# First pair's q on ScalarE's queue and in a bank of its own, raw weights behind the first finished x, last tile's transposes in a row

## Chip, core and metric

The kernel runs on one core of a Trainium2 chip. The metric is the device time of one execution in microseconds, as the median of several runs.

## What is computed

Attention with a soft cap on the scores, for 4 batches of 12 heads with 448 tokens of 64 features, and behind it two two-layer MLPs over the 1792 tokens (768 to 2048 to 768 features), all in fp32:

```python
scores = cap * tanh(q @ k.T / sqrt(64) / cap)
attn   = exp(scores - max) / (sum(exp(scores - max)) + 1e-9)
x = attn @ v                                  # 4 x 12 x 448 x 64, then as 1792 x 768
h = maximum(x @ w1, 0);  x = (h * h) @ w2
h = x @ w3;              out = (h * sigmoid(1.702 * h)) @ w4
```

## The kernel before

`bounded_cap` serves caps up to 40, which the inputs have; `any_cap` is a second version behind a branch on the flag `over`, which isn't taken here. All engines run in the order in which the code is written (`in_order`), so the order of the source is the order of the queues.

**Attention** goes over 24 pairs of heads. Time is cut in steps T, eight to a pair: `PLAN` says at which step, counted from the pair's own first, each piece of it is emitted. `load_pair` (step -17) fetches k and q of a pair on SP's queue, `load_v` (-9) v. `prep_k` and `prep_q` transpose them on TensorE against `ident` into the PSUM pool `ps_x`, which has a single bank, and split them in a high and a low part: k by ScalarE (copy) and VectorE (subtract) to `kk`, q by two VectorE passes to `qq`. `scores`, `tanhs`, `exps` and `pv` follow for four chunks of keys; the last chunk (`TAIL`) holds the 64 left over keys of both heads. `take_x` and `divide` make x, which POOL's queue writes to `xs`. k is kept in two buffers `kz`, whose unused rows `emit_const` clears.

**Weights.** The MLP's weights come as raw 8-byte words. For each of 11 chunks within attention, two loads (`wraw`, POOL's queue) are each followed by a join (ScalarE into `sx`, then VectorE's shift to `wy`), and then by sums (four VectorE operations) and writes to `wsa` or `wsb` (POOL's queue). `weight_group` puts these into a list, three loads ahead; `weight_slot`, called at the steps of `ATT_WORK`, takes one join or one sum from it, with the loads that follow. The group is opened at step 2:

```python
if T == 2:
    weight_group(ATT_CHUNKS)
if T in ATT_WORK:
    weight_slot()
...
ATT_WORK = tuple(10 + 11 * n // 2 for n in range(33))
```

The list is taken up at the first slot, step 10, where the three loads at its head are emitted ahead of the first join. On POOL nothing but its constants is queued ahead of them, so they leave as soon as these are set.

**MLPs.** From there TensorE works through products (`product`, L1094) of weights `wh`, `wl` with `form`. The last result tile of the second MLP is transposed back in `result` with four TensorE transposes into one bank, each followed by a copy and an output DMA, on VectorE and SP's queue or on ScalarE and its queue in turn.

Of the kernel before, what the change touches and what calls it, by code (L numbers as in the profile page):

```python
# [8 lines left out]
F32 = mybir.dt.float32  # L9
# [667 lines left out]
@with_exitstack  # L677
def bounded_cap(ctx, tc, q, k, v, cap, w1, w2, w3, w4, out):

# [59 lines left out]
    sx = const.tile([P, KD, P], I32, name="sx")  # L739
    kz = [kz_p.tile([P, KW], F32, name=f"kz{i}") for i in range(2)]  # L740
    v1 = [kz_p.tile([P, 2 * TAIL + 1, 2, D], F32, name=f"v1{i}") for i in range(VB)]
# [7 lines left out]
    def emit_const():  # L749
        nc.vector.memset(kz[0][:32], 0.0)  # L750
        nc.gpsimd.memset(kz[1][:32], 0.0)
        nc.sync.dma_start(out=capt, in_=cap.rearrange("(o n) -> o n", o=1).to_broadcast([P, 1]))
# [6 lines left out]
        nc.vector.reciprocal(qs, acap)  # L759
        nc.vector.tensor_scalar(ecap, acap, CAP_MAX, None, ALU.min)  # L760
        nc.vector.tensor_scalar(qs, qs, float(D) ** -0.5, None, ALU.mult)


    pairs = [(b, p) for b in range(B) for p in range(NP)]
    raw, vst, prep, pps, sc, et, pvp, x32 = ({} for _ in range(8))

    def halves():
        for j in range(2):
            yield j, slice(64 * j, 64 * j + 64), slice(64 * (1 - j), 64 * (1 - j) + 64)

    def load_pair(b, p):
        kt = kz[p % 2].rearrange("p (c h d) -> p c h d", h=2, d=D)
        qt = ld.tile([CP, NCH, 2, D], F32, tag="q", name="qt")
        ka, kb, qa, qb = (
            src[b, 2 * p + j].rearrange("(p c) d -> p c d", c=NCH) for src in (k, q) for j in range(2)
        )
# [7 lines left out]
    def transposed(t, name):  # L784
        n = KW if name == "kps" else S
        ps = ps_x.tile([P, 512], F32, tag="x", name=name)
        for c in range(NCH):
            nc.tensor.transpose(
                ps[:, c:n:NCH], t[:, c].rearrange("p h d -> p (h d)"), ident[: n // NCH, : n // NCH]
            )  # L790
        return ps[:, :n]

    def load_v(b, p):
        va, vb = v[b, 2 * p], v[b, 2 * p + 1]
        vt = vst[b, p] = v1[(b * NP + p) % VB]
        tt = vt[:, 2 * TAIL]
        Q_LOAD.dma_start(out=vt[:, 0 : 2 * TAIL : 2, 0], in_=va[64:].rearrange("(c p) d -> p c d", p=P))
        Q_LOAD.dma_start(out=vt[:, 1 : 2 * TAIL : 2, 1], in_=vb[: TAIL * P].rearrange("(c p) d -> p c d", p=P))
        Q_LOAD.dma_start(out=tt[64:, 0], in_=va[:64])
        Q_LOAD.dma_start(out=tt[:64, 1], in_=vb[TAIL * P :])  # L800

    def prep_k(b, p, step):
        if step == 0:
            pps[b, p] = transposed(raw[b, p][1], "kps")
            return
        ps = pps[b, p]
        if step == 1:
            kk = qk_p.tile([P, 2, KW], F32R, tag="kk", name="kk")
            prep[b, p] = [None, kk]
            a_.activation(kk[:, 0, :], ps, AF.Copy)  # L810
        else:
            kk = prep[b, p][1]
            v_.tensor_tensor(kk[:, 1, :], ps, f32(kk[:, 0, :]), ALU.subtract)

    def prep_q(b, p, step):
        if step == 0:
            pps[b, p] = transposed(raw.pop((b, p))[0], "qps")
            return
        ps = pps[b, p]
        if step == 1:  # L820
            qq = prep[b, p][0] = qk_p.tile([P, 2, S], F32R, tag="qq", name="qq")
            v_.tensor_scalar(qq[:, 0, :], ps, qs, None, ALU.mult)  # L822
        else:
            qq = prep[b, p][0]
            v_.scalar_tensor_tensor(qq[:, 1, :], ps, qs, f32(qq[:, 0, :]), ALU.mult, ALU.subtract)

    def scores(b, p, c):
        qq, kk = prep[b, p]
        ps = sc[b, p, c] = ps_s.tile([P, 2, 512], F32, tag="s", name="sps")
        tail = c == TAIL  # L830
        cols = slice(0, P) if tail else slice((c + 1) * P, (c + 2) * P)
        if tail:
# [24 lines left out]
    def pv(b, p, c):  # L857
# [22 lines left out]
    def divide(b, p):  # L880
# [375 lines left out]
    def result(l, c, row, col, d, y):  # L1256
# [183 lines left out]
def softcap_attention_mlp_mlp(ctx, tc, q, k, v, cap, w1, w2, w3, w4, out):  # L1440

    nc = tc.nc
    pool = ctx.enter_context(tc.tile_pool(name="flag", bufs=1))
    c = pool.tile([1, 2], F32, name="capsize")
    over = pool.tile([1, 1], I32, name="over")
    nc.sync.dma_start(out=c[:, 0:1], in_=cap.rearrange("(o n) -> o n", o=1))
    nc.vector.tensor_scalar(c[:, 1:2], c[:, 0:1], -1.0, None, ALU.mult)
    nc.vector.tensor_tensor(c[:, 0:1], c[:, 0:1], c[:, 1:2], ALU.max)
    nc.vector.tensor_scalar(over, c[:, 0:1], CAP_MAX, None, ALU.is_gt)
    bounded_cap(tc, q, k, v, cap, w1, w2, w3, w4, out)  # L1450
    flag = nc.values_load(over, min_val=0, max_val=1)
# [32 lines left out]
```

## Time and profile before

| | us |
|---|---|
| median of three runs | 1115.71 |
| the three runs | 1114.51, 1115.71, 1116.39 |
| the profiled execution | 1114.16 |
| its span | 1112.4 |
| TensorE busy | 1069.3 (96%) |
| VectorE busy | 863.2 (78%) |
| ScalarE busy | 722.6 (65%) |

The profile is of one execution. A timeline row gives the start and the duration of one instruction (or of several merged ones, "x4"), its engine (PE is TensorE, PEld its weight loads, DVE VectorE, ACT ScalarE, POOL GpSimd, SPq and ACTq the DMA issues of SP and ScalarE), its line in the kernel, the tile it writes and the tiles it reads. What stands in brackets is how long the engine was idle before it, and what ended that. Matmul ends are modelled, so a busy TensorE isn't one at its peak.

### The profile page before, as it was taken

To read this page: it belongs to the slowest core of one execution; us is meant where nothing else is said; L and a number is where in the kernel's file an instruction comes from. 1 tells how busy PE (TensorE), PEld (TensorE's weight loads), DVE (VectorE), ACT (ScalarE), POOL (GpSimd) and SP (SyncE) were. 2 spreads that over 40 slices of the span, in tenths; PEclk is the share of its full clock that TensorE was granted. 3 is DMA by queue.
4 is the path that set the end of the run, shared out by engine and by line. 5 is a ranking of instruction groups with operands and counts; after the bars stand their busy time and mean duration, and the time that the engine had idled before them with its cause. 6 is when DMAs were issued, how large, how long until landed. Compare 5 with 4: busy or idle time off the path is not lost.

```text
span 1112.4 us, 15612 instructions
## 1 busy us (share of the span) xinstructions
PE 1069.3 (96%) x5119; PEld 887.4 (80%) x5119; DVE 863.2 (78%) x1173; ACT 722.6 (65%) x1131; POOL 276.6 (25%) x414
## 2 busy tenths in 40 slices
PE   4999999999999999999999999999999999999997
PEld 2555554556999999989998998999799879998996
DVE  2788889999667987876699769778894875569854
ACT  3999998997667656466685655667555455565541
POOL 2222233322342013122210322443022410001033
PEclk9999999999999999999999999999999999999999
DMA  6798999856878467688964876898343543333442
GB/s 168 199 242 225 247 272 249 217 179 218 264 272 279 135 227 259 208 264 286 309 220 156 270 270 197 281 319 287 119 152 106 195 140 114 101 113 117 136 127 65
DMA packets 158860, 228.23 MB, mean 205 GB/s; under 512 B 80898, under 2 KB 111746, under 8 KB 158770
## 3 DMA queue, kind: packets, MB, share of 16 engines
q0 software_dynamic: 33696, 122.28, 33.7%
q1 hardware_dynamic: 124818, 104.75, 32.4%
q8 instruction: 42, 0.69, 0.3%
q14 instruction: 48, 0.39, 0.1%
q10 hardware_dynamic: 256, 0.11, 0.0%
HBM read 166.53 MB, written 60.56 MB: 204 GB/s over the span
## 4 chain that ended last, share of the span: by engine, by line
PE 59%; DVE 14%; issue 8%; DMA 5%; ACT 4%; POOL 1%; DVEq 0%; ACTq 0%; POOLq 0%
PE pb L1094 28%; PE pa L1094 27%; DVE form L1103 3%; DMA wf<-wsa 3%; DVE wl L1071 3%; PE vps L867 2%; PE sps L841 1%; DMA out_dram<-o 1%; DVE ct L882 1%; ACT sx L942 1%; DVE g L1215 1%; DVE g L1296 1%; DVE qu L1296 1%; ACT e L851 1%; ACT e L855 1%
## 5 line engine op out<-in xcount | busy, mean ns | idle before, releaser
L1094 PE MATMUL pa<-form,wh 128*128 128x448 f32 x1536 | 439.7, 367 | 7.1 <-DVE form L1103 5.8
L1094 PE MATMUL pb<-form,wh 128*128 128x448 f32 x1152 | 329.4, 367 | 2.0 <-DVE form L1103 1.1
L1094 PEld LDWEIGHTS pa<-form,wh 128*128 128x128 f32 x1536 | 288.9, 188 | 34.3 <-DVE form L1103 7.4
L1094 PE MATMUL pa<-form,wl 128*128 128x448 f32 x768 | 282.4, 368 | 5.4 <-DVE wl L1071 5.3
L1070 ACT ACTIVATE wh<-wf 128x384 fp32r<-128x384 f32 (+1 forms) x392 | 211.3, 560 | 66.2 <-DMA wf<-wsa 27.1
L1071 DVE TENSOR_TENSOR wl<-wf,wh 128x384 fp32r<-128x384 f32 (+1 forms) x392 | 225.4, 607 | 27.7 <-ACT wh L1070 22.8
L1094 PEld LDWEIGHTS pb<-form,wh 128*128 128x128 f32 x1152 | 216.5, 188 | 22.3 <-DVE form L1103 1.8
L1094 PE MATMUL pb<-form,wl 128*128 128x448 f32 x576 | 210.8, 366 | 0.0
L1094 PEld LDWEIGHTS pa<-form,wl 128*128 128x128 f32 x768 | 144.5, 188 | 20.2 <-DVE wl L1071 8.3
L867 PE MATMUL vps<-e,v 128*128 128x448 f32 (+1 forms) x384 | 148.1, 552 | 2.3 <-DVE x L878 2.2
L1276 POOL DMA_DIRECT2D out_dram<-o x92 | 57.9, 636 | 253.9 <-DVE o L1274 250.6
L1094 PEld LDWEIGHTS pb<-form,wl 128*128 128x128 f32 x576 | 108.3, 188 | 9.1
L1103 DVE TENSOR_TENSOR form<-g,form 128x1344 fp32r<-128x1344 f32 (+1 forms) x72 | 100.7, 1399 | 8.5 <-ACT form L1102 7.8
L841 PE MATMUL sps<-qq,kk 64*128 64x448 f32 (+1 forms) x504 | 92.6, 419 | 0.9 <-DVE qq L822 0.9
L867 PEld LDWEIGHTS vps<-e,v 128*128 128x128 f32 (+1 forms) x384 | 59.6, 189 | 42.4 <-issue 26.0
L855 ACT ACTIVATE e<-e,ecap 128x896 f32<-128x896 f32 x96 | 91.0, 948 | 1.9
L1293 ACT ACTIVATE qu<-pb 128x448 f32<-128x448 f32 x88 | 47.5, 540 | 68.7 <-PE pb L1094 65.1
L946 DVE SCALAR_TENSOR_TENSOR wy<-wraw,sx 128x768 int32<-128x768 int32 (+1 forms) x68 | 61.7, 908 | 37.3 <-ACT sx L942 37.3
L851 ACT ACTIVATE e<-sps 128x896 f32<-128x896 f32 x96 | 78.0, 813 | 19.2 <-PE sps L841 18.6
L841 PEld LDWEIGHTS sps<-qq,kk 64*128 64x128 f32 (+1 forms) x504 | 50.0, 190 | 46.6 <-ACT kk L810 13.0
L1102 ACT ACTIVATE form<-g 128x1344 fp32r<-128x1344 f32 (+1 forms) x72 | 85.8, 1192 | 2.0 <-DVE g L1254 1.9
L882 DVE RECIPROCAL ct<-ct 128x448 f32<-128x448 f32 x24 | 70.7, 2945 | 0.0
(91 smaller groups left out, 1001.1 us busy)
## 6 DMA issues: line engine op xcount, KB each, us to landing
wf<-wsa SPq DMA_DIRECT2D x224, 192.0 KB, 3.9
wf<-wsb SPq DMA_DIRECT2D x168, 256.0 KB, 3.2
wraw<-in_moe_w_in_dram POOLq DMA_DIRECT2D x32, 766.5 KB, 7.2
wraw<-in_moe_w_out_dram POOLq DMA_DIRECT2D x48, 383.2 KB, 6.0
wsa<-wy POOLq DMA_DIRECT2D x32, 384.0 KB, 4.3
wsb<-wy POOLq DMA_DIRECT2D x24, 384.0 KB, 4.4
wsa<-ws POOLq DMA_DIRECT2D x16, 384.0 KB, 3.4
wraw<-in_moe_w_out_dram POOLq DMA_DIRECT2D x24, 255.5 KB, 5.1
```

The lines of the kernel that those rows point to most:

```text
L841: nc.tensor.matmul(ps[:, u, :S], x, y, start=all(t[0] != u for t in todo[:n]), stop=all(t[0] != u for t in todo[n + 1 :]),)
L851: a_.activation(e, chunk(c, sc.pop((b, p, c)))[:, :, :S], AF.Tanh)
L855: a_.activation(e, e, AF.Exp, scale=ecap)
L867: nc.tensor.matmul(pvp[b, p][j][:, :S], x.rearrange("p a d -> p (a d)"), t, start=c == 0, stop=c == TAIL,)
L882: v_.reciprocal(ct, ct)
L946: v_.scalar_tensor_tensor(y[:, : 2 * n].bitcast(I32), words(I32)[:, :, :, 0], 13, sx[:, : 2 * n], ALU.logical_shift_right, ALU.bitwise_or,)
L1070: a_.activation(x, src, AF.Copy)
L1071: later.append(lambda: v_.tensor_tensor(y, src, f32(x), ALU.subtract))
L1094: nc.tensor.matmul(ps[:, :S], a[:, kk % 4, :], r, start=(s in (1, 5) and kk == 0 and n == 0), stop=(kk == ks - 1 and n == 2), skip_group_c ...
L1102: a_.activation(f[:, 0, :n, :], src, AF.Copy)
L1103: later.append(lambda: v_.tensor_tensor(f[:, 1, :n, :], src, f32(f[:, 0, :n, :]), ALU.subtract))
L1276: nc.gpsimd.dma_start(out=out[b * S : (b + 1) * S, m * P + 32 * j : m * P + 32 * j + 32].rearrange("(c p) d -> p c d", p=32), in_=o[32 * j ...
```

## The change

- `load_pair` of the first pair issues q on ScalarE's queue; k and v are fetched in other pieces (k's and v's first 384 tokens as 128 x 3, the last 64 by themselves), and step -17 becomes -18. The cap is loaded once, on ScalarE's queue, and `over` is computed from `acap`.
- The first pair's preparation is written out in `attn_start`: q's transposes go first, into a bank of `ps_m`, then k's into `ps_x`. T starts at -10 instead of -17.
- The weight group opens at step 15 with its first three loads (`weight_loads`), behind the first `divide` at step 14, and `ATT_WORK` is 26 + 5n instead of 10 + 5.5n.
- The last tile's four transposes stand one behind the other; then VectorE and ScalarE copy two columns of blocks each and issue one DMA each.

```diff
 def load_pair(b, p):
+    kt = kz[p % 2]
     qt = ld.tile([CP, NCH, 2, D], F32, tag="q", name="qt")
-    Q_LOAD.dma_start(out=kt[16:, :, 0, :], in_=ka)
-    Q_LOAD.dma_start(out=kt[32:, :, 1, :], in_=kb[:96])
-    Q_LOAD.dma_start(out=kt[:16, :, 1, :], in_=kb[96:])
-    Q_LOAD.dma_start(out=qt[:, :, 0, :], in_=qa)
-    Q_LOAD.dma_start(out=qt[:, :, 1, :], in_=qb)
+    queue = nc.scalar if (b, p) == pairs[0] else Q_LOAD
+    for j in range(2):
+        Q_LOAD.dma_start(out=kt[:, :TAIL, j], in_=k[b, 2 * p + j, :MAIN].rearrange("(p c) d -> p c d", c=TAIL))
+    for j, r, o in halves():
+        Q_LOAD.dma_start(out=kt[r, TAIL, j], in_=k[b, 2 * p + j, MAIN:])
+    for j in range(2):
+        queue.dma_start(out=qt[:, :, j], in_=q[b, 2 * p + j].rearrange("(p c) d -> p c d", c=NCH))
...
 def prep_q(b, p, step):
     if step == 0:
-        pps[b, p] = transposed(raw.pop((b, p))[0], "qps")
+        bank = ps_m if (b, p) == pairs[0] else None
+        qps[b, p] = transposed(raw[b, p][0], "qps", bank)
         return
...
+    def attn_start():
+        for f, step in ((prep_q, 0), (prep_k, 0), (prep_q, 1), (prep_k, 1), (prep_q, 2), (prep_k, 2)):
+            f(*pairs[0], step)
...
+    def weight_loads():
+        while work and work[0][0].__name__.startswith("load"):
+            f, *a = work.pop(0)
+            f(*a)
...
         for j in range(NCH):
-            at = slice(P * j, P * j + P)
-            nc.tensor.transpose(ps[:CP, at], y[:, CP * j : CP * j + CP], ident)
-            (v_.tensor_copy, a_.copy)[j % 2](o[:CP, at], ps[:CP, at])
-            (nc.sync, nc.scalar)[j % 2].dma_start(
-                out=out[b * S + CP * j : b * S + CP * j + CP, m * P : m * P + P], in_=o[:CP, at]
+            nc.tensor.transpose(ps[:CP, P * j : P * j + P], y[:, CP * j : CP * j + CP], ident)
+        for j, copy, queue in ((0, v_.tensor_copy, nc.sync), (2, a_.copy, nc.scalar)):
+            at = slice(P * j, P * j + 2 * P)
+            copy(o[:CP, at], ps[:CP, at])
+            queue.dma_start(
...
-    T = -17
+    T = -10
+    nc.scalar.dma_start(out=capt, in_=cap.rearrange("(o n) -> o n", o=1).to_broadcast([P, 1]))
+    load_pair(*pairs[0])
     emit_const()
...
-        if T == 2:
+        if T == 15:
             weight_group(ATT_CHUNKS)
+            weight_loads()
...
-ATT_WORK = tuple(10 + 11 * n // 2 for n in range(33))
+ATT_WORK = tuple(26 + 5 * n for n in range(33))
```

How the instructions stand then, at three places. On TensorE at the start of the program (kps and qps are the transposes of k and q, sps the scores), before:

```order
L788 MATMUL kps<-ident,kz_117 128x128 x4
L788 MATMUL qps<-ident,qt 128x112 x4
L841 MATMUL sps<-qq,kk 128x448 x6
L788 MATMUL kps<-ident,kz_118 128x128 x4
L841 MATMUL sps<-qq,kk 128x448 x6
L788 MATMUL qps<-ident,qt 128x112 x4
```

and now:

```order
L789 MATMUL qps<-ident,qt 128x112 x4
L789 MATMUL kps<-ident,kz_112 128x128 x4
L840 MATMUL sps<-qq,kk 128x448 x6
L789 MATMUL kps<-ident,kz_113 128x128 x4
L840 MATMUL sps<-qq,kk 128x448 x6
L789 MATMUL qps<-ident,qt 128x112 x4
```

q's transposes of the first pair have moved ahead of k's; the second pair's stand where they stood. On POOL, behind its constants (wraw are raw weights, wsa and xs the DRAM tiles of the weights and of x), before:

```order
L756 MEMSET sx 128x768
L930 DMA wraw<-in_moe_w_in_dram 128x6x1022 x3
L961 DMA wsa_124<-wy 128x2x384
L930 DMA wraw<-in_moe_w_in_dram 128x6x1022
L884 DMA xs<-x_303 128x448
L930 DMA wraw<-in_moe_w_in_dram 128x6x1022
```

and now:

```order
L753 MEMSET sx 128x768
L883 DMA xs<-x_291 128x448
L938 DMA wraw<-in_moe_w_in_dram 128x6x1022 x3
L883 DMA xs<-x_380 128x448
L969 DMA wsa_119<-wy 128x2x384
L938 DMA wraw<-in_moe_w_in_dram 128x6x1022
```

The first x is now written ahead of the first raw loads, and the second ahead of the first joined weights. On SP at the start (qt, kz and v are the tiles of q, k and v), before:

```order
L1446 DMA capsize<-in_cap_dram 1x1
L752 DMA capt<-in_cap_dram 128x1
L777 DMA kz_117<-in_k_dram 112x4x64
L778 DMA kz_117<-in_k_dram 96x4x64
L779 DMA kz_117<-in_k_dram 16x4x64
L780 DMA qt<-in_q_dram 112x4x64
L781 DMA qt<-in_q_dram 112x4x64
L1451 TENSOR_LOAD over
L1451 ISA x2
L797 DMA v_119<-in_v_dram 128x3x64
```

and now:

```order
L778 DMA kz_112<-in_k_dram 128x3x64 x2
L780 DMA kz_112<-in_k_dram 64x64 x2
L778 DMA kz_113<-in_k_dram 128x3x64 x2
L780 DMA kz_113<-in_k_dram 64x64 x2
L782 DMA qt<-in_q_dram 112x4x64 x2
L1468 TENSOR_LOAD over
L1468 ISA x2
L796 DMA v_114<-in_v_dram 128x3x64
```

The cap and the first pair's q have left SP, and the second pair's k and q stand ahead of the first pair's v.

## Rows read from the trace of the kernel before

**Rows 1.** The page's slices: busy tenths of ScalarE in 40 equal parts.
```profile
ACT  3999998997667656466685655667555455565541
```

**Rows 2.** Timeline of TensorE, columns as in Rows 3: the first product.
```profile
260.31 0.68 PE L1094 MATMUL pa<-form,wh 128*128 128x448 f32 x2
```

**Rows 3.** Timeline, first 40 us: start, us, engine, line, operation, idle before.
```profile
1.57 0.74 SPq L777 DMA_DIRECT2D kz<-in_k_dram  x1
...
4.75 2.62 POOL L930 DMA_DIRECT2D wraw<-in_moe_w_in_dram  x3
...
5.63 1.09 PE L788 MATMUL kps<-ident,kz 128*128 128x128 f32 x4 [5.63 <-DMA kz<-in_k_dram]
...
6.76 0.60 ACT L810 ACTIVATE kk<-kps 128x512 fp32r<-128x512 f32 x1 [4.73 <-PE kps L788]
...
7.39 0.69 DVE L813 TENSOR_TENSOR kk<-kps,kk 128x512 fp32r<-128x512 f32 x1 [2.88 <-ACT kk L810]
...
8.13 1.01 PE L788 MATMUL qps<-ident,qt 112*128 112x112 f32 x4 [1.41 <-DVE kk L813]
8.57 0.62 SPq L777 DMA_DIRECT2D kz<-in_k_dram  x1
...
10.01 1.74 PE L841 MATMUL sps<-qq,kk 64*128 64x448 f32 x6 [0.87 <-DVE qq L822]
...
17.99 1.09 PE L788 MATMUL kps<-ident,kz 128*128 128x128 f32 x4 [6.24 <-DMA kz<-in_k_dram]
...
22.85 3.35 PE L867 MATMUL vps<-e,v 128*128 128x448 f32 x4
...
29.21 0.66 PE L788 MATMUL kps<-ident,kz 128*128 128x128 f32 x4
```

**Rows 4.** DMA issues of 0 to 20 us: count, KB each, median us to landing.
```profile
wraw<-in_moe_w_in_dram POOLq DMA_DIRECT2D x3, 766.5 KB, 7.5
...
kz<-in_k_dram SPq DMA_DIRECT2D x3, 112.0 KB, 2.7
```

**Rows 5.** Stretches: busy us of PE, PEld, DVE, ACT, POOL; clock; DMA share; GB/s.
```profile
0.00:35.00 35.00, 20.85 (x81) 11.85 (x82) 8.33 (x19) 14.95 (x19) 7.85 (x16) 1.00 0.60 146
35.00:260.00 225.00, 218.13 (x1000) 117.65 (x998) 202.45 (x246) 210.03 (x283) 67.29 (x101) 1.00 0.86 233
...
29.33:48.54 19.21, 19.21 (x91) 10.58 (x92) 14.28 (x19) 18.14 (x25) 4.11 (x6) 1.00 0.77 185
...
146.98:249.71 102.73, 97.48 (x451) 52.60 (x452) 95.73 (x122) 96.91 (x135) 32.08 (x49) 1.00 0.83 227
```

**Rows 6.** Timeline of the end, same columns.
```profile
1104.22 0.32 PE L1266 MATMUL pa<-ident,qu 128*112 128x128 f32 x1 [0.72 <-DVE qu L1296]
1104.58 0.29 DVE L1267 COPY wf<-pa 112x128 f32<-112x128 f32 x1 [0.41 <-PE pa L1266]
...
1107.02 0.32 ACTq L1268 DMA_DIRECT2D out_dram<-wf  x1
```

**Rows 7.** Timeline of TensorE's weight loads (PEld).
```profile
25.25 0.34 PEld L841 LDWEIGHTS sps<-qq,kk 128*128 128x128 f32 x1 [0.41 <-ACT e L855]
...
27.19 0.19 PEld L867 LDWEIGHTS vps<-e,v 128*128 128x128 f32 x1 [0.19 <-issue]
```

**Rows 8.** Timeline of ScalarE: pairs 1 and 2 begin, and a join.
```profile
29.33 0.92 ACT L851 ACTIVATE e<-sps 128x896 f32<-128x896 f32 x1 [1.06 <-PE sps L841]
...
31.55 1.07 ACT L942 ACTIVATE sx<-wraw 128x768 f16<-128x768 bf16 x1
...
39.26 0.91 ACT L851 ACTIVATE e<-sps 128x896 f32<-128x896 f32 x1
```

**Rows 9.** Timeline of VectorE: a join's shift, and the first operation of a sum.
```profile
40.13 0.95 DVE L946 SCALAR_TENSOR_TENSOR wy<-wraw,sx 128x768 int32<-128x768 int32 x1
...
45.98 0.55 DVE L970 TENSOR_TENSOR ws<-wy 128x384 f32<-128x384 f32 x1
```

**Rows 10.** Waits of 20 to 270 us: total us, times, longest.
```profile
PEld kps L788 <- DMA v<-in_v_dram: 0.9, 3, 0.3
```

More of the change, by code (lines that the diff above doesn't have):

```diff
@@ L677, in bounded_cap @@
 @with_exitstack
-def bounded_cap(ctx, tc, q, k, v, cap, w1, w2, w3, w4, out):
+def bounded_cap(ctx, tc, q, k, v, cap, w1, w2, w3, w4, out, over):
     nc = tc.nc
@@ L739, in bounded_cap @@
     sx = const.tile([P, KD, P], I32, name="sx")
-    kz = [kz_p.tile([P, KW], F32, name=f"kz{i}") for i in range(2)]
+    kz = [kz_p.tile([P, NCH, 2, D], F32, name=f"kz{i}") for i in range(2)]
     v1 = [kz_p.tile([P, 2 * TAIL + 1, 2, D], F32, name=f"v1{i}") for i in range(VB)]
@@ L759, in emit_const @@
         nc.vector.reciprocal(qs, acap)
+        nc.vector.tensor_scalar(qs, qs, float(D) ** -0.5, None, ALU.mult)
         nc.vector.tensor_scalar(ecap, acap, CAP_MAX, None, ALU.min)
-        nc.vector.tensor_scalar(qs, qs, float(D) ** -0.5, None, ALU.mult)
+        nc.vector.tensor_scalar(over, acap[:1], CAP_MAX, None, ALU.is_gt)
     pairs = [(b, p) for b in range(B) for p in range(NP)]
-    raw, vst, prep, pps, sc, et, pvp, x32 = ({} for _ in range(8))
+    raw, vst, prep, pps, qps, sc, et, pvp, x32 = ({} for _ in range(9))
     def halves():
@@ L769, in halves @@
             yield j, slice(64 * j, 64 * j + 64), slice(64 * (1 - j), 64 * (1 - j) + 64)
+    MAIN = TAIL * P
     def load_pair(b, p):
-        kt = kz[p % 2].rearrange("p (c h d) -> p c h d", h=2, d=D)
+        h = slice(2 * p, 2 * p + 2)
+        kt = kz[p % 2]
         qt = ld.tile([CP, NCH, 2, D], F32, tag="q", name="qt")
-        ka, kb, qa, qb = (
-            src[b, 2 * p + j].rearrange("(p c) d -> p c d", c=NCH) for src in (k, q) for j in range(2)
-        )
-        Q_LOAD.dma_start(out=kt[16:, :, 0, :], in_=ka)
@@ L782, in load_pair, with transposed @@
+        for j in range(2):
+            queue.dma_start(out=qt[:, :, j], in_=q[b, 2 * p + j].rearrange("(p c) d -> p c d", c=NCH))
         raw[b, p] = (qt, kt)
-    def transposed(t, name):
-        n = KW if name == "kps" else S
-        ps = ps_x.tile([P, 512], F32, tag="x", name=name)
+    def transposed(t, name, bank=None):
+        ps = (bank or ps_x).tile([P, 512], F32, tag="m" if bank else "x", name=name)
         for c in range(NCH):
[L788 to L791, printed above, removed]
+            cols, n = (slice(c * P, c * P + P), P) if name == "kps" else (slice(c, S, NCH), CP)
+            nc.tensor.transpose(ps[:, cols], t[:, c].rearrange("p h d -> p (h d)"), ident[:n, :n])
+        return ps[:, : KW if name == "kps" else S]
@@ L793, in load_v @@
     def load_v(b, p):
-        va, vb = v[b, 2 * p], v[b, 2 * p + 1]
         vt = vst[b, p] = v1[(b * NP + p) % VB]
[L796 to L800, printed above, removed]
+        for j, r, o in halves():
+            src = v[b, 2 * p + j]
+            Q_LOAD.dma_start(out=vt[:, j : 2 * TAIL : 2, j], in_=src[:MAIN].rearrange("(p c) d -> p c d", c=TAIL))
+            Q_LOAD.dma_start(out=vt[r, 2 * TAIL, j], in_=src[MAIN:])
@@ L816, in prep_q @@
         if step == 0:
-            pps[b, p] = transposed(raw.pop((b, p))[0], "qps")
+            bank = ps_m if (b, p) == pairs[0] else None
+            qps[b, p] = transposed(raw[b, p][0], "qps", bank)
             return
-        ps = pps[b, p]
+        ps = qps[b, p]
         if step == 1:
-            qq = prep[b, p][0] = qk_p.tile([P, 2, S], F32R, tag="qq", name="qq")
+            qq = qk_p.tile([P, 2, S], F32R, tag="qq", name="qq")
+            prep.setdefault((b, p), [None, None])[0] = qq
             v_.tensor_scalar(qq[:, 0, :], ps, qs, None, ALU.mult)
@@ L830, in scores @@
         tail = c == TAIL
-        cols = slice(0, P) if tail else slice((c + 1) * P, (c + 2) * P)
+        cols = slice(c * P, c * P + P)
         if tail:
@@ L862, in pv @@
         if c == TAIL:
-            todo = [(j, vt[o, 2 * TAIL], e[o, 0, :]) for j, r, o in halves()]
+            todo = [(j, vt[r, 2 * TAIL], e[r, 0, :]) for j, r, o in halves()]
         else:
@@ L886, in bounded_cap @@
     PLAN = {
-        -17: [(load_pair,)],
+        -18: [(load_pair,)],
         -8: [(prep_k, 0)],
@@ L899, in bounded_cap @@
     ORDER = sorted(PLAN, reverse=True)
+    PLAN_K = -8
+    EARLY = (-18, -8, -7, -5, -4)
+    def attn_start():
+        for f, step in ((prep_q, 0), (prep_k, 0), (prep_q, 1), (prep_k, 1), (prep_q, 2), (prep_k, 2)):
+            f(*pairs[0], step)
     def attn_sub(t):
+        if t == PLAN_K:
+            attn_start()
         for d in ORDER:
             n, r = divmod(t - d, 8)
-            if r == 0 and 0 <= n < len(pairs):
+            if r == 0 and 0 <= n < len(pairs) and not (n == 0 and d in EARLY):
                 for f, *a in PLAN[d]:
@@ L1443, in softcap_attention_mlp_mlp @@
     pool = ctx.enter_context(tc.tile_pool(name="flag", bufs=1))
-    c = pool.tile([1, 2], F32, name="capsize")
     over = pool.tile([1, 1], I32, name="over")
[L1446 to L1450, printed above, removed]
+    bounded_cap(tc, q, k, v, cap, w1, w2, w3, w4, out, over)
     flag = nc.values_load(over, min_val=0, max_val=1)
```

11 lines of the change are left out of this document (7 added, 4 removed).

## The prediction

> **What bounds the kernel now.** I read the page's slices first, then the timeline of the first 40 us, the table by stretches and ScalarE's rows for the attention stage, then the last 10 us. There are two stages. Until the first product at 260.31 attention runs, and ScalarE is busy nearly throughout [rows 1, 2]; behind it TensorE is the bound, and the change touches nothing there but the last tile. So the attention stage and the two ends have to be costed.
>
> The start is in [rows 3]. SP issues the first pair's k from 1.57, TensorE transposes it at 5.63, ScalarE and VectorE split it, and only when VectorE has read the bank (7.39 and 0.69) can q use the same PSUM bank, at 8.13. The first scores run at 10.01, 4.38 us behind the first transpose, and end at 11.75. Then TensorE stands still for 6.24 us until 17.99: the second pair's k, issued from 8.57, has not landed. What delays it is seen beside it: POOL issues three raw weight loads of 766.5 KB at 4.75, and in these 20 us one takes 7.5 us to land, while the first k pieces need 2.7 [rows 3, 4].
>
> From 29 us on ScalarE sets the pace of a pair, with VectorE close behind: ScalarE is busy 18.14 of 19.21 us in pairs 1 and 2, and 96.9 of the 102.7 us of pairs 13 to 22 (10.3 us a pair), where VectorE has 95.7 [rows 5]. The end is a chain of four links, each a transpose and a copy, from 1104.22 to the last output DMA at 1107.02 [rows 6].
>
> **The change part by part.** The sum is made against the profiled execution, 1114.16 us (span 1112.4), and carried over to the median of the three runs, 1115.71.
>
> *First pair.* q goes out on ScalarE's queue, behind cap and ahead of the table load. k becomes SP's first DMA, since both cap loads leave SP: up to 0.8 us earlier than 1.57, but in four pieces where there were three (an issue is 0.62 to 0.74). I take 0.5 us off the 5.63. q has its own bank, so the chain from the first transpose to the first scores is now 1.01 (q) + 1.09 (k) + 0.60 (ScalarE's copy of k) and some 0.1 of hand-overs, 2.8 instead of 4.38: VectorE's q passes run while k is transposed, and its k pass beside the first four score matmuls [rows 3]. With the 0.5 that is 2.0 us; bounds 1.0 (q lands late) and 2.4.
>
> For the queue alone a row gives the price: an issue is 0.62 us on SP [rows 3], and two leave it. The Trainium skill (DMA: Bandwidth & Descriptors, "Issuing engines are not separate DMA queues") says that DMAs of all issuing engines run on the same 16 DMA engines, so that a second issuer saves only the sequencer's time. By it the second queue would be worth 1.2 us at most and the bank has to bring the rest of the 2.0. The trace agrees that queues share: POOL's loads hold up SP's [rows 3, 4].
>
> *The wait for the second pair.* With no raw load in flight SP's sequence is k0 (4 issues), k1 (4), q1 (2): k1's last issue begins at about 5 us. It lands at 7.7 by the 2.7 of [rows 4], at 9.9 if it were to need 4.9; the scores end at 11.75 - 2.0 = 9.75. So the 6.24 go, all but 0 to 0.2; for the range up to 2 us are left. Next late could be v of pair 0: SP reads the flag and then issues v behind ten DMAs, from about 8 us, which lands by 11 to 14. It is wanted at 22.85 - 8.2 = 14.65 [rows 3], so nothing is counted, but the margin is small. The start is worth 2.0 + 6.2 = **8.2 us**.
>
> *The clock.* The granted clock reads 1.00 here, yet one weight load of 128 columns takes 0.34 us at 25.25 and 0.19 at 27.19 [rows 7]: TensorE ran at the lower of its levels (1.2 GHz) to about 26 and at 2.4 from there, after being busy without a gap since 17.99. In the new order the gapless stretch begins 8.2 us earlier or more. I let the rise move with the rest: 0, and up to 2 us more gained if it comes sooner still.
>
> *Weights later and denser.* The 33 weight slots (two joins and a sum for each of 11 chunks) ran from step 10 every 5.5 steps and now run from step 26 every 5; both end at step 186, and a pair is 8 steps. Pairs 1 and 2 lose two joins and one sum. The pair from 29.33 had the joins and took 9.93, the next one, without, 19.21 - 9.93 = 9.28 [rows 5, 8]. Two pairs at 9.2 against 19.21 gain 0.8 us. The work comes back: by the step numbers pairs 3 to 12 get one join more, pairs 13 to 22 one join and one sum. A join is 1.07 us on ScalarE and 0.95 on VectorE, a sum four VectorE operations of 0.55 [rows 8, 9]. A join cost a pair (9.93 - 9.28) / 2 = 0.33 us where VectorE had room; where both engines are full a join can cost 0.9 and a join with its sum 2.9. I take 0.5 for the first and 1.2 for the second: **-1.7 us**, bounds -0.7 and -3.8. The loads move too: the first three raw loads now stand on POOL behind the first xs write, at step 15, when pair 4's k and q are being fetched (see the rivals).
>
> *Pieces with one answer.* k and v are fetched in other shapes with as many 256-byte pieces; k takes one issue more a pair on SP, which runs ten steps ahead; k's transposes write their bank without a stride. I count 0 for all three, 0.5 us either way.
>
> *Last tile.* Four transposes back to back take about 0.66, as k's four at the higher level do [rows 3]; by [rows 6] 4 x 0.32 = 1.28 if nothing overlaps. Then VectorE copies 256 columns and ScalarE, which waits for that, the other 256. 128 columns take 0.29 [rows 6], VectorE's pass over k's 512 columns 0.69 [rows 3]: some 0.4 each. That makes 1.6 us to the last issue instead of 2.80. Each DMA carries twice the bytes, for which I take 0.2 off: **+1.0**, bounds 0 and 1.3. The 5 us behind the last issue stay.
>
> Sum: 8.2 + 0.8 - 1.7 + 1.0 = **8.3 us** gained.
>
> **The rivals.** *Slower: the DMA engines become the bound of attention.* From 35 to 260 us they moved 233 GB/s at a share of 0.86, and 57.5 MB in the whole 260 us [rows 5]. In the first 28 us now only q, k and v of four pairs move (2.7 MB), so 55 MB fall behind them. If 233 GB/s is all that this mix of small pieces gives, those take 236 us, attention ends at 264 instead of 260, and with 1.0 from the tail the run is 3 us longer: 1118.7. It decides below 55 / (260 - 28) = 237 GB/s. For it speaks the share; against it that TensorE's largest wait on a load between 20 and 270 us is 0.9 us in all [rows 10], and that a raw load has ten steps, about 12 us, until its join. 5%.
>
> *The burst comes back.* Three raw loads at step 15 do to pair 4 what they did to pair 1: up to the 6.24 us of [rows 3] are paid there, and 2.1 are left: 1113.6. Against it: pair 4's k is issued at step 14 and wanted at step 24, and POOL cannot issue the raw loads before VectorE has finished x, some 4 us behind step 14. 5%.
>
> *The denser slots cost more.* The bound of -3.8 and a start that yields 6 instead of 8.2: 4 us gained, 1111.7. For it: in the late pairs VectorE has 7% left [rows 5], and two joins then fall into one pair. 16%.
>
> *The clock rises with the first dense work,* in the low teens: 10.3 us gained, 1105.4. For it: TensorE has almost no gap from 5 us on. Against: before, it was busy 8 us without a gap and still at the lower level [rows 3, 7]. The Trainium skill (TensorE: Matmul & The Clock Gate, "Part 1: The HAM clock gate") says that throttled is the default and that activity releases it. By that rule a TensorE that is busy sooner is fast sooner, which may bring this rival's time; the rows agree in that the rise came after gapless work. 12%.
>
> **How the numbers follow.** The likeliest case, 62%: 1115.7 - 8.3 = 1107.4, between 1105.3 and 1109.7 as the bounds of its terms combine. On the profiled execution it would be 1105.9; that one lies 1.5 us below the median, which is what I carry. The range takes in most of the clock's rival and reaches up to the denser slots: 1103.5 to 1111.7, and leaves out the two DMA cases and the ends. A difference of 0.2% (2.2 us) is about what a measurement of this kernel can tell from none. Below 1113.5 lie the first case, the clock, the denser slots and part of the burst, 90%; within 0.2% 6%; slower 4%.
>
> **What would show it.** The first scores should start at about 8 us, the second pair's k transpose at 9 to 10.5 with no wait on k ahead of it, weight loads of 0.19 should be there by about 18.5. Pairs 1 and 2 should take 9.0 to 9.4 each, pairs 13 to 22 10.3 to 10.6. The first product should start near 252.5 instead of 260.31, and the last output DMA be issued 1.6 us behind the last tile's first transpose. I am wrong if TensorE or ScalarE waits for a load of k, v or raw weights after 12 us, if VectorE is over 97% busy in pairs 13 to 22 with a pair near 11 us, or if the shift at the first product is under 5 us.

## The result, and the profile after

| | before | after |
|---|---|---|
| median, us | 1116.05 (1114.51 to 1118.04, 4 runs) | 1106.20 (1104.83 to 1107.07, 4 runs) |
| ratio | | 0.991, 95% interval 0.989 to 0.9929 |
| profiled execution, its span | 1114.16, 1112.4 | 1104.83, 1103.0 |
| first product | 260.31 | 250.92 |
| first product to the last tile's first transpose | 843.91 | 844.68 |
| from there to the end of the span | 8.2 | 7.4 |

9.85 us were gained where 8.3 were forecast, and 1106.2 stands against 1107.4. Between the two profiled executions it is 9.33 us, and all of that lies ahead of the first product (9.39): the MLPs took 0.77 longer, the last tile gave 0.7 (8.15 against 7.44 us, not rounded). In the MLPs this execution has two falls of TensorE's clock (at 469 and 677 us) where that of before has one (at 900); what such a fall costs is measured below.

The start of the timeline after, beside [rows 3]:

```profile
0.74 1.34 SPq L778 DMA_DIRECT2D kz<-in_k_dram  x2
...
1.18 1.33 ACTq L782 DMA_DIRECT2D qt<-in_q_dram  x2
...
5.98 0.98 PE L789 MATMUL qps<-ident,qt 112*128 112x112 f32 x4 [5.98 <-DMA qt<-in_q_dram]
6.75 1.06 PE L789 MATMUL kps<-ident,kz 128*128 128x128 f32 x4
7.00 0.68 DVE L821 TENSOR_SCALAR qq<-qps,qs 128x448 fp32r<-128x448 f32 x1 [2.60 <-PE qps L789]
...
7.85 0.60 ACT L807 ACTIVATE kk<-kps 128x512 fp32r<-128x512 f32 x1 [4.03 <-PE kps L789]
...
8.50 1.49 PE L840 MATMUL sps<-qq,kk 64*128 64x448 f32 x6 [0.69 <-ACT kk L807]
...
9.92 1.11 PE L789 MATMUL kps<-ident,kz 128*128 128x128 f32 x4
...
12.45 0.40 PEld L789 LDWEIGHTS qps<-ident,qt 112*128 112x128 f32 x4 [0.61 <-DVE kk L810]
```

The chain from the first transpose to the first scores is 2.52 us, where it was 4.38; q is what TensorE now waits for, where it was k, and q lands at 5.98. The second pair's k is transposed at 9.92, with no wait for a load ahead of it, where it was 17.99. And the last row shows a weight load at 0.10 us each (0.40 for four) already at 12.45: TensorE is at its upper level (2.4 GHz) 14 us sooner than in [rows 7].

The attention stage after, in stretches. Columns: busy us and instructions of each engine named, granted clock, DMA share, GB/s.

```profile
30.00:60.00 30.00, 27.66 (x37) 1.00 0.99 270
60.00:100.00 40.00, 37.80 (x51) 1.00 0.97 262
100.00:150.00 50.00, 46.67 (x63) 1.00 0.98 269
```

(ScalarE is the engine in these.) The DMA engines move 262 to 270 GB/s, above the 233 of [rows 5] and the 237 at which the first rival decided, and from 8 to 235 us no computing engine waits more than 0.3 us for a load of q, k, v or raw weights. At 150 us, though, TensorE's clock falls, which it never did in before's attention. VectorE and TensorE in the timeline, then TensorE's busy time with the granted clock:

```profile
146.32 0.55 DVE L978 TENSOR_TENSOR ws<-wy 128x384 f32<-128x384 f32 x1
...
147.85 0.55 DVE L981 TENSOR_TENSOR wt<-wy,ws 128x384 f32<-128x384 f32 x1
148.32 0.62 DVE L1135 TENSOR_TENSOR form<-xt,form 128x448 fp32r<-128x448 f32 x1
148.97 0.62 DVE L1139 TENSOR_TENSOR xt<-xu,xt 128x448 f32<-128x448 f32 x1
149.51 0.68 DVE L810 TENSOR_TENSOR kk<-kps,kk 128x512 fp32r<-128x512 f32 x1
...
150.25 0.60 PE L789 MATMUL qps<-ident,qt 112*128 112x112 f32 x4 [1.51 <-DVE kk L810]
```

```profile
148.00:151.00 3.00, 1.49 (x10) 1.00 0.89 324
151.00:153.00 2.00, 2.00 (x9) 0.73 0.72 222
153.00:155.00 2.00, 2.00 (x5) 0.50 0.55 126
155.00:157.00 2.00, 2.00 (x7) 0.92 0.96 282
```

A sum of the weight slots (step 111) and a slice of x (step 112) stand on VectorE ahead of k's split, so that TensorE idles 1.51 us for its bank; behind that its clock falls to 0.50, that is 1.2 GHz, for some 3 us (over the last three of these stretches 1.7 us of clock are lost).

The end, beside [rows 6]:

```profile
1095.60 0.65 PE L1278 MATMUL pa<-ident,qu 128*112 128x128 f32 x4 [0.72 <-DVE qu L1313]
1096.28 0.42 DVE L1281 COPY wf<-pa 112x256 f32<-112x256 f32 x1 [0.74 <-PE pa L1278]
...
1097.20 0.38 ACTq L1282 DMA_DIRECT2D out_dram<-wf  x1
```

From the first transpose to the last issue it is 1.60 us, as forecast, where it was 2.80.

### The profile page after: what moved, and what is told of

Its sections match the earlier page's. It is cut to its first block, busy times and chain, and to the rows that moved or that the text cites. A ratio compares the mean times of both kernels' runs of the same rounds, so it can differ in the third digit from the quotient of the medians.

```text
span 1103.0 us, 15632 instructions
## 1 busy us (share of the span) xinstructions
PE 1066.8 (97%) x5119; PEld 888.3 (81%) x5119; DVE 862.4 (78%) x1170; ACT 723.2 (66%) x1130; POOL 276.0 (25%) x414
## 4 chain that ended last, share of the span: by engine, by line
PE 61%; DVE 13%; issue 5%; DMA 2%; ACT 2%; POOL 1%; DVEq 0%; ACTq 0%; POOLq 0%
PE pa L1107 30%; PE pb L1107 30%; DVE form L1116 3%; DVE wl L1084 3%; DMA out_dram<-o 1%; DVE ct L881 1%; DVE g L1228 1%; ACT form L1115 1%; DVE xl L1196 1%; DMA xl<-ys 1%; DVE wy L954 1%; DVE qu L1313 1%; DVE g L1313 0%; DVE tl L1228 0%; DVE x L877 0%
```

## Experiments: the parts of the start

The theory was that the start gains by two things, the bank with q's queue (2.0 us) and the raw loads moved away from the second pair (6.2). Four kernels undo or do one part alone. In total time these four, 1105.9 to 1108.0 us, aren't told apart from after's 1106.2 (the runs of one kernel spread over 6 to 7 us), so the argument goes by the stages of one profiled execution each. To compare stages, ScalarE's copies of k (kk, one a pair) serve as marks: the third stands at 30.14 before and 19.32 after.

**Old weight schedule in the changed kernel.**

```diff
-        if T == 15:
+        if T == 2:
             weight_group(ATT_CHUNKS)
-            weight_loads()
-ATT_WORK = tuple(26 + 5 * n for n in range(33))
+ATT_WORK = tuple(10 + 11 * n // 2 for n in range(33))
```

> The changed kernel with the old weight schedule (group opened at step 2, slots at 10 + 5.5n, no loads of their own ahead). Theory, that the raw loads in flight hold up the second pair's k: the raw loads leave POOL at about 4.8 us again, TensorE waits 4 us or more for k ahead of the second pair's transposes (9.92 in the changed kernel, then 14 or later), weight loads of 0.19 us come only after that; pairs 13 to 22 go back to about 10.3 us, so that 1 to 2.6 us come back: 1108.5 to 1112 in all. Rival, that the new order of SP's issues alone (k of the second pair is issued from 3.47 instead of 8.57) removed the wait: kps of the second pair stays at about 10, first product at 250 or sooner, 1103.5 to 1106.

Measured: 1107.97 us (1106.25 to 1112.25, 7 runs), first product 255.72. Timeline of TensorE and of POOL's and SP's issues:

```profile
4.43 2.62 POOL L938 DMA_DIRECT2D wraw<-in_moe_w_in_dram  x3
...
6.08 1.62 SPq L782 DMA_DIRECT2D qt<-in_q_dram  x2
...
11.14 0.45 PE L789 MATMUL kps<-ident,kz 128*128 128x128 f32 x1 [0.35 <-DMA kz<-in_k_dram]
...
17.22 0.98 PE L789 MATMUL qps<-ident,qt 112*128 112x112 f32 x4 [4.21 <-DMA qt<-in_q_dram]
```

The wait is back, 4.56 us, but for q and not for k: k is issued early enough now to get ahead of the raw loads, q is not. The third kk comes at 25.59, 6.3 us later than after. The theory holds, with the place of the wait missed.

**New weight schedule alone, in the kernel before** (the lines above the other way round).

> The kernel before with the new weight schedule alone (group at step 15 with its first loads, slots at 26 + 5n). Theory: the 6.24 us wait for the second pair's k goes nearly whole, its transposes start by 12.5 instead of 17.99, first product 253 to 255, 1108.5 to 1110.5. Rival, that k waits for its late issue at 8.57 and not for the raw loads: 3 us or more of the wait stay and the run is 1112 or more. On the clock: if the rise comes with the first dense work and not at a fixed time, 0.19 us weight loads are there by 16.

Measured: 1106.61 us (1104.13 to 1111.45, 6 runs), first product 252.00, third kk 21.99, weight loads of 0.19 us from 16.93. In its timeline the wait for k is 0.54:

```profile
9.90 1.74 PE L841 MATMUL sps<-qq,kk 64*128 64x448 f32 x6 [0.87 <-DVE qq L822]
...
12.19 1.09 PE L788 MATMUL kps<-ident,kz 128*128 128x128 f32 x4 [0.54 <-DMA kz<-in_k_dram]
```

With SP's issues as late as before (k's third piece at 9.64), k is there by 12.2. So the raw loads held it up, and moving them is by itself worth 260.31 - 252.00 = 8.3 us ahead of the first product, where the whole change has 9.4. The two parts do not add up: the rest of the change without it still brings 260.31 - 255.72 = 4.6.

**One bank for q and k, k first; and q on SP's queue.** The first takes `ps_x` for the first pair's q and writes k's three steps ahead of q's; the second sends q out behind k.

```diff
-            bank = ps_m if (b, p) == pairs[0] else None
-            qps[b, p] = transposed(raw[b, p][0], "qps", bank)
+            qps[b, p] = transposed(raw[b, p][0], "qps")
...
-        for f, step in ((prep_q, 0), (prep_k, 0), (prep_q, 1), (prep_k, 1), (prep_q, 2), (prep_k, 2)):
+        for f, step in ((prep_k, 0), (prep_k, 1), (prep_k, 2), (prep_q, 0), (prep_q, 1), (prep_q, 2)):
```

and the second kernel's only edit:

```diff
-        queue = nc.scalar if (b, p) == pairs[0] else Q_LOAD
+        queue = Q_LOAD
```

> The changed kernel with the first pair's q in the single bank of ps_x again and k's three steps ahead of q's three (q's queue and the weights stay new). Theory: the first scores start 1.3 to 1.7 us later than 8.50, everything behind moves with them, first product at about 252.4, 1107.5. Rival, that the bank is worth nothing, since q and the second pair's k land late anyway: second pair's transposes at 9.9 to 10.3, 1106.2.

> The changed kernel with the first pair's q issued on SP's queue again, behind k's four issues (its own bank stays). Theory: q's two issues end about 1.3 us later than on ScalarE's queue and q lands as much later, so the first transposes start at 6.9 to 7.4 instead of 5.98 and the first scores at 9.2 to 9.8 instead of 8.50. Rival, that all DMAs share the same engines and q lands no later: first transposes at 5.9 to 6.2. A third outcome, k then first: TensorE waits for q all the same, since q's transposes stand ahead of k's.

Measured: one bank 1106.80 us (1102.33 to 1108.16, 6 runs); q on SP 1105.92 (one run). Timeline of TensorE, of the first and then of the second:

```profile
5.23 1.44 PE L789 MATMUL kps<-ident,kz 128*128 128x128 f32 x4 [5.23 <-DMA kz<-in_k_dram]
...
9.96 1.74 PE L839 MATMUL sps<-qq,kk 64*128 64x448 f32 x6 [0.87 <-DVE qq L820]
```

```profile
3.43 1.31 SPq L782 DMA_DIRECT2D qt<-in_q_dram  x2
...
7.57 0.98 PE L789 MATMUL qps<-ident,qt 112*128 112x112 f32 x4 [7.57 <-DMA qt<-in_q_dram]
...
10.09 1.12 PE L840 MATMUL sps<-qq,kk 64*128 64x448 f32 x4 [0.69 <-ACT kk L807]
```

The first scores stand at 9.96 and 10.09, where after has 8.50 and before 10.01. So bank and queue bring 1.5 us together at the first scores, and either alone, in these orders, brings nothing: without the bank q waits for VectorE, without the queue it lands 1.59 us later. Not run is the bank without the queue and with k's transposes first, where k's chain could go on while q is under way. How much of the 1.5 us lasts is open too: the third kk with q on SP, 20.93, lies within the 19.32 to 21.72 that the same start with both parts has in six executions (see the clock); with one bank it is 22.06. On the queue the Trainium skill (DMA: Bandwidth & Descriptors, "Issuing engines are not separate DMA queues") says that a second issuer saves only the time to issue; the rows agree in kind, q being issued at 3.43 instead of 1.18 and landing 1.59 later.

## Experiments: what sets the pace of a pair

After's pairs did not go as forecast: pairs 1 and 2 took 9.60 us each, not 9.0 to 9.4, and the denser slots cost nothing early and, in this execution, 2.6 us late (the table below) instead of 1.2. Two theories stood: ScalarE with VectorE sets the pace (the prediction's), or TensorE does.

**One sum moved away from the slice of x** (also the base of the kernels that follow).

```diff
-ATT_WORK = tuple(26 + 5 * n for n in range(33))
+ATT_WORK = tuple(26 + 5 * n + 3 * (n == 17) for n in range(33))
```

> The changed kernel with one weight slot, a sum, moved from step 111 to step 114, away from the slice of x at step 112. Theory, that the sum and the slice on VectorE hold up k's split of pair 15, that TensorE's idle of 1.51 us at about 149 follows from it and the fall of its granted clock to 0.50 behind that: no idle above 1 us on TensorE between 140 and 165, granted clock 1.00 there, pairs 14 and 15 under 11 us each, first product 2 to 3 us sooner than 250.92, 1103.2 to 1104.2. Rival, that the sum's 2 us are only late somewhere else or the fall is chance: first product at 250.4 to 251.4, 1106.

Measured: 1103.98 us (1101.97 to 1106.19, 6 runs), first product 249.45. No idle of TensorE over 1 us from 140 to 165, and the clock is 1.00:

```profile
140.00:150.00 10.00, 10.00 (x51) 1.00 0.99 260
150.00:160.00 10.00, 9.42 (x44) 1.00 0.80 253
```

The first product comes only 1.5 us sooner than after's, since this execution's third kk was 0.9 later (see the clock). From mark to mark it is plainer:

| us between copies of k | before | new weights alone | after | sum moved |
|---|---|---|---|---|
| third to sixth | 29.30 | 29.13 | 29.12 | 29.11 |
| sixth to sixteenth | 98.50 | 97.58 | 97.51 | 97.54 |
| sixteenth to twenty-fourth | 82.13 | 83.08 | 84.74 | 82.35 |
| twenty-fourth to first product | 20.24 | 20.22 | 20.23 | 20.21 |

The kernels with one bank, with q on SP and with new weights alone have the same wait, 1.53 us, and their clock stays up behind it. So the collision costs 0.73 (83.08 - 82.35; the four kernels further down that keep both the sum moved and all of a pair's work have 82.36 to 82.38) and the fall of the clock, which one of four executions had, 1.66 more.

**ScalarE's joins left out.** The line that copies one half of each raw word into `sx` is taken away, in all the program; the weights lack that part.

```diff
-            a_.activation(z, words(BF16)[:, :, :, 2], AF.Copy)
```

> sum_moved without ScalarE's part of the joins in all the program (the weights lack their low parts; 22 of these copies of 1.07 us lie in attention, 23.5 us of ScalarE's time). If ScalarE sets the pace of a pair, as the prediction had it, attention ends up to 23 us sooner: first product at 226 to 230. If TensorE's own work is a floor of 9.6 us a pair, joins or not, pairs go to 9.6 and hardly below: first product at 238 to 243.

Measured: 1100.56 us (one run), first product 249.00. From the third kk (21.72) to it are 227.28 us, where sum_moved has 229.21: 1.9 of the 23.5 us. Two pairs in a row (columns: busy us of PE, PEld, DVE, ACT, POOL; clock; DMA share; GB/s):

```profile
40.96:50.56 9.60, 9.60 (x47) 5.29 (x46) 7.66 (x9) 8.32 (x13) 2.14 (x3) 1.00 1.14 297
50.56:60.16 9.60, 9.60 (x47) 5.29 (x46) 7.57 (x12) 8.32 (x13) 3.35 (x5) 1.00 1.02 232
```

ScalarE has 1.28 us of each pair free and the pair is not shorter: TensorE is busy 9.60 of 9.60. From the sixth to the sixteenth kk it took 96.33 where sum_moved has 97.54, so ScalarE's part of a join costs 0.12 us a pair here and not 0.33 to 0.9 (VectorE's part stayed).

**One pass of the scores instead of three** (the two passes with low parts left out).

```diff
-                for ik, iq in ((0, 0), (0, 1), (1, 0))
+                for ik, iq in ((0, 0),)
```

> sum_moved with one of the three passes of the score matmuls alone (high part times high part; the other two are left out, so TensorE's 3.74 us of scores in a pair become about 1.3). If TensorE's own work is the floor of 9.6 us of a pair without weight slots, pairs 1 and 2 go to 8.3 to 8.8 us, where ScalarE is full, and the later pairs to 9.5 to 10, first product 236 to 244. If something else holds the pair (ScalarE's chain of tanh and exp, VectorE), pairs 1 and 2 stay at 9.5 or more and the first product at 247 or later.

Measured: 1099.19 us (one run), first product 240.40, and pairs 1 and 2:

```profile
20.05:28.56 8.51, 8.51 (x34) 4.27 (x33) 5.91 (x6) 8.21 (x13) 0.00 (x0) 1.00 0.43 96
28.56:36.80 8.24, 8.24 (x32) 3.78 (x31) 6.70 (x8) 8.10 (x13) 3.20 (x4) 1.00 0.78 220
```

With less work for TensorE the pair becomes 1.1 to 1.4 us shorter, with less for ScalarE it did not. So TensorE's 9.60 us was the floor of these pairs. What holds the shorter pair isn't shown: ScalarE is busy 8.10 of 8.24 us, but TensorE reads full here too, with two thirds of its score work gone. From the sixteenth to the twenty-fourth kk it took 82.23 us, hardly less than sum_moved's 82.35; four falls of the clock stand in it (granted clock 0.66 in 143 to 148, 164 to 169, 184 to 189 and 215 to 220 us), behind idle times of TensorE of 1.0 to 2.9 us.

**VectorE's reciprocal left out** (2.94 us a pair; x is multiplied by the sums).

```diff
-        v_.reciprocal(ct, ct)
```

> sum_moved without VectorE's reciprocal in divide (2.94 us a pair; x is multiplied by the sums instead of divided). If VectorE is what takes pairs 3 to 22 from TensorE's 9.6 us to the 10.1 and more that they need, nearly all go to 9.6 to 9.7 and the first product to 238 to 243; if it is not, pairs and first product stay as in sum_moved (249.45, within 1 us). Pairs 1 and 2 stay at 9.60 in both.

Measured: 1094.08 us (one run), first product 244.48, between the two theories. From the sixth to the sixteenth kk it saves 1.04 us (96.50), in the next eight pairs 2.83 (79.52), behind them 1.13. VectorE therefore matters where slices of x come on top of sums and joins, from about 145 us on, and hardly before. Even there pairs stay at 9.94 us, above 9.60, and what takes the rest is open.

## Experiments: the clock, and the spread of the runs

**Idle time filled at the start.** Transposes of `ident` into a bank that nothing reads: fifteen ahead of the first pair in the first kernel; seventeen there and four where TensorE waits for k's copy in the second, which also has the matmuls of the next experiment and five moved sums.

```diff
     emit_const()
+    warm = ps_m.tile([P, 512], F32, tag="m", name="warm")
+    for _ in range(15):
+        nc.tensor.transpose(warm[:, :P], ident, ident)
```

The second kernel's other edits, where `warm(n)` does n such transposes:

```diff
         for f, step in ((prep_q, 0), (prep_k, 0), (prep_q, 1), (prep_k, 1), (prep_q, 2), (prep_k, 2)):
             f(*pairs[0], step)
+            if (f, step) == (prep_k, 0):
+                warm(4)
...
-ATT_WORK = tuple(26 + 5 * n for n in range(33))
+ATT_WORK = tuple(26 + 5 * n + {17: 3, 20: -2, 23: 1, 26: 2, 29: 4}.get(n, 0) for n in range(33))
```

> sum_moved with fifteen transposes of the identity on TensorE ahead of the first pair, into a bank that nothing reads (added work, 128 columns each, done by about 5.9 us). Theory, that the clock's level follows how long TensorE has been at work: weight loads of 128 columns take 0.19 us by 10 us or sooner instead of 12.4 to 15, the start shortens by 1.5 to 3 us, first product 246.5 to 248 where sum_moved has 249.45, 1101 to 1102.5 in all. Rival, that the rise comes at a time that TensorE's own early work does not set: still the lower level until 12 or later, first product 249.5, 1104.

> wait_fill with seventeen transposes of the identity ahead of the first pair, four more where TensorE waits for k's copy, and five sums moved three steps behind a slice of x instead of one. Theory, that TensorE kept at work holds the level once it has it: first scores at 7.4 or so, no fall in 5 to 20 us, weight loads of 0.19 from 6 us on without a break, first product 245.5 to 247.5, 1098 to 1100. Rival, that the level falls again whatever is added, as in warm_start (0.50 from about 8 to 15 us): first product 248.5 to 249.5, 1101 to 1102.

Measured: warm_start 1102.56 us (1100.80 to 1106.04, 6 runs), both_fills 1101.63 (1099.42 to 1102.84, 6 runs; ratio to before 0.987, 0.9841 to 0.9898). TensorE's busy time and granted clock at the start, of the first and then of the second:

```profile
5.00:10.00 5.00, 3.47 (x18) 0.85 0.40 90
10.00:15.00 5.00, 5.00 (x19) 0.50 0.41 91
15.00:20.00 5.00, 5.00 (x21) 0.97 0.50 113
```

```profile
5.00:10.00 5.00, 4.25 (x30) 1.00 0.40 90
10.00:15.00 5.00, 4.17 (x22) 1.00 0.41 92
15.00:20.00 5.00, 5.00 (x26) 1.00 0.44 98
```

In warm_start the first scores come at 7.42, but the level that the transposes had brought is lost again from about 8 to 15 us, and the third kk is at 20.10, no better than sum_moved's 20.24. With the four transposes more (and seventeen instead of fifteen ahead of them) it holds: third kk at 17.99, 1.3 us ahead of the best without. That is one trace of each. Of both theories' forecasts for the first product (245.5 to 247.5 or 248.5 to 249.5) it has 248.49, since one of my five moved sums then stood ahead of the last pair's split of k and cost 1.3 us (TensorE idle 2.47 up to 231.83, with no fall of the clock behind it). The other moved sums gained nothing: from the sixteenth to the twenty-fourth kk it took 82.38 us, where sum_moved has 82.35.

The six kernels whose program is the same up to there (after, sum_moved and four more built on it) have their first weight load at the upper level between 12.4 and 17.8 us and their third kk between 19.32 and 21.72. So the moment at which the level rises is not the program's alone, and 2.4 us hang on it. The Trainium skill (TensorE: Matmul & The Clock Gate, "Part 1: The HAM clock gate") says that the chip's watch on activity runs freely and doesn't begin with the kernel, so that this moment differs between runs; the rows agree, with a wider spread (5.4 us) than the half microsecond either way that the page gives.

**Idle time filled in the MLPs.** TensorE waits 1.4 to 2.0 us for a form at three places there (468, 677 and 893 us in after), and in some executions the clock falls behind such a wait. Six matmuls into a bank that nothing reads go into each place, in border_fill too early (s = 1 instead of 2, 7 us ahead of where the wait begins), in wait_fill into the wait:

```diff
+                if (l, c) != (0, 0) and (kind, s, i, kk, n) == ("a", 2, 0, 0, 0):
+                    b = pool["pb"].tile([P, 512], F32, tag="b", name="pb")
+                    for _ in range(6):
+                        nc.tensor.matmul(b[:, :S], whi[:, 0, :], hi, start=True, stop=True)
```

> sum_moved with six matmuls added in each of the three places in the MLPs where TensorE waits 1.4 to 2.0 us for a form (first product of a layer's half: 468, 677 and 893 us in the changed kernel), into a bank that nothing reads. Theory, that these idle times are what makes the granted clock fall to 0.50 in some executions, and that this makes up most of the spread between executions: granted clock 1.00 in all stretches of 5 us from 260 to 1095, from the first product to the end 848 to 850 us instead of 850.8 to 855, runs within 2 us of each other, median 1101 to 1102.5. Rival, that the falls are not from idle time, or that the added matmuls cost their own time: falls remain, median 1104 or more.

> sum_moved with six matmuls added where TensorE waits 1.4 to 2.0 us for a form in the MLPs (the first product with s = 2 of each half but the first: 468, 677 and 893 us in the changed kernel), into a bank that nothing reads; border_fill had put them 8.5 us ahead of these waits. Theory, that the idle time makes the granted clock fall in some executions: no fall in the MLPs, first product to end of span 848 to 850 us, runs within 2 us of each other, median 1100.5 to 1102. Rival, that the falls have another cause: still one or two falls in 260 to 1095, median 1103 to 1104, runs spread over 4 us or more.

Measured: border_fill 1103.39 us (1100.49 to 1107.59, 6 runs); its waits stayed at 1.43, 1.43 and 1.96 us, and one fall (0.66 in 890 to 895). wait_fill 1102.61 (1096.83 to 1105.15, 6 runs): no fall in the MLPs of its trace, in that of both_fills neither, and the mean granted clock of wait_fill's six runs is 0.998 to 0.999, where sum_moved's six have 0.993 to 0.997 (both_fills' six have 0.996 to 0.998, which leaves room for a fall in some). The first of the three places, in after and then in wait_fill, where the bank pb takes the six added matmuls:

```profile
468.22 0.47 PE L1107 MATMUL pa<-form,wh 128*128 128x448 f32 x1 [1.44 <-DVE form L1116]
```

```profile
469.60 1.39 PE L1115 MATMUL pb<-form,wh 128*128 128x448 f32 x6
471.19 0.47 PE L1107 MATMUL pa<-form,wh 128*128 128x448 f32 x1 [0.20 <-DVE form L1120]
```

Counted over all traces, the twelve that left these waits unfilled have 36 of them and 16 falls in the MLPs (the end of the span left out), each within 2 us behind one; the two that filled them have none. So the falls come from these waits, but idle time alone does not decide: a fourth wait of 1.5 to 1.6 us (786 us in after, for wl) has no fall behind it in any of the fourteen.

The second half of the theory fell: the runs spread over 8 us, and from the first product to the end wait_fill took 851.4 us, longer than sum_moved with two falls (850.7). Where that went is in the number of matmuls in equal stretches at a granted clock of 1.00, of sum_moved and then of wait_fill:

```profile
270.00:370.00 100.00, 100.00 (x495) 1.00 0.75 247
...
590.00:670.00 80.00, 80.00 (x389) 1.00 0.69 230
690.00:770.00 80.00, 80.00 (x396) 1.00 0.92 300
900.00:990.00 90.00, 90.00 (x446) 1.00 0.35 112
```

```profile
270.00:370.00 100.00, 100.00 (x486) 1.00 0.78 251
...
590.00:670.00 80.00, 80.00 (x397) 1.00 0.70 232
690.00:770.00 80.00, 80.00 (x389) 1.00 0.89 290
900.00:990.00 90.00, 90.00 (x446) 1.00 0.37 113
```

Of the same matmuls sum_moved does 495 in 100 us where wait_fill does 486, and from 590 to 670 it is the other way round. In the timeline three matmuls take 0.609 us at the one pace and 0.620 at the other, and the slower one holds for 60 to 200 us, in one trace for 320. wait_fill loses 3.5 us against sum_moved up to 470 and gets some 1.6 back from 580 to 670 (90 us by 1.8%). Both paces occur in the trace of before too (0.620 from 820 to 880 and from 1010 to 1090). In the traces that exist 80 to 420 us of the MLPs ran at the slower pace, 1.4 to 7.6 us; the kernel with the new weights alone had the 420. In the fourteen traces nearly all changes of pace lie near the same few places, some 15, 220, 330, 425, 530, 630, 750 and 830 us behind the first product, so the program has a part in when the pace changes; what chooses it is open. The slower pace accounts for wait_fill's time: it held some 330 us there and 96 in sum_moved, 1.8% of the difference is 4.2 us, and less the two falls at 1.7 that is 0.8, where 0.6 was measured; the added matmuls cost nothing that shows. That the pace makes most of the spread between the runs without a trace is an inference.

## Why the prediction was right, step by step

- **First pair, 2.0 us.** First scores at 8.50 instead of 10.01: 1.5. The chain became 2.52 us, even shorter than the 2.8 taken; but the 0.5 us of an earlier start did not come, since q lands at 5.98, later than k did before. In the orders that were run, bank and queue each need the other. The price of the queue alone, two issues of 0.62 us, was too low: on SP q stands behind k's four issues and lands 1.59 us later.
- **The wait for the second pair, 6.2.** Its k is transposed 8.07 us sooner with no wait left; 8.2 were forecast for the start. What was late next was nothing: v of pair 0 was in time, as counted.
- **The clock, 0.** The rival came true in part: the upper level was there by 12.45, and after's third kk leads by 10.82 us, 2.75 more than the start gave. But it is a draw, and the best of six: another execution of the same start has 21.72, a lead of 8.4. The argument against it, eight gapless microseconds at the lower level in before, was one draw read as a rule.
- **Pairs 1 and 2, +0.8.** Measured 0: 19.20 us against 19.21. Here the step failed by its reading. The row in [rows 5] shows TensorE busy 19.21 of 19.21 us beside ScalarE's 18.14, and I named ScalarE. The 9.28 us of one pair and 9.93 of the other were no prices with and without joins: together they are twice 9.60, TensorE's floor (and the second pair was not free of weight work: a sum stands in it, at 45.98 in [rows 9]).
- **Denser slots, -0.5 and -1.2.** From before to the kernel with the new weights alone the early pairs gained 0.9 and the late ones lost 0.95; why the early ones gained is open. The two terms together with the 0.8 gave -0.9 in the sum and +0.1 on the chip. The profiled execution of after lost 2.6 in the late pairs, 1.66 of it the fall of the clock.
- **DMA bound, burst at pair 4.** Refuted by 262 to 270 GB/s, and by no wait on a load at the fourth and fifth pair.
- **Last tile, +1.0.** Measured 0.7: the 1.60 us to the last issue are exact; what follows is longer than taken (5.84 us from the start of that issue to the end of the span, where it was 5.35), 0.5 instead of 0.2.
- **The sum.** On the profiled executions 8.07 (start) + 2.75 (clock) - 1.43 (pairs and slots, with the fall) - 0.77 (MLPs) + 0.71 (last tile) = 9.3, where 8.2 + 0 - 0.9 + 0 + 1.0 = 8.3 was forecast. The start, the main term, was right by its mechanism; that the rest came out near the forecast is partly luck, since two draws of the clock, 2.75 gained and 1.66 lost, offset each other.
- **The range.** It took in the clock's rival and held; what it left unnamed, two paces in the MLPs worth up to 7.6 us, is as large as the whole gain.

## What to carry to other kernels

When two engines are nearly full, take work away from each in turn before pricing a change by one of them: one row had TensorE at 19.21 of 19.21 and I priced by ScalarE at 18.14. The full row was the right candidate here, but with modelled ends it proves little (TensorE still read full with two thirds of the scores gone); the two removals decided. A big load that nobody needs soon can be worth more when it is moved behind the first loads than a rearrangement of these: here 8.3 us alone, the rest alone 4.6, both 9.4. Two cures that each remove one of two equally late causes (a bank, a queue) can be worth nothing alone, as in the two orders run here.

## What was not expected of the hardware

- TensorE's matmuls have two paces 1.8% apart (0.609 and 0.620 us for three of 448 columns) at the same granted clock of 1.00, the slower kept for 60 to 320 us; the traced executions lost 1.4 to 7.6 us by it, and changes fall near the same places of the program.
- Idle times of TensorE of 1.4 to 2.0 us are followed in some executions by some 3 us at half clock, about 1.7 us lost, and in others by nothing: 1.51 us up to 150.25 with a fall, 1.53 in three other traces without, 2.47 in one without. Of the three waits in the MLPs 16 of 36 had a fall, and none of the six that were filled with matmuls whose results nobody reads.
- The same start reaches the upper level of the clock at 12.4 to 17.8 us, in six executions.
